# Row dot products on VectorE for a fifth of the w2 and wo blocks, and output 0 moved into the w1 products

## The chip, the cores and the metric

One core of one Trainium2 chip. Times are device microseconds (us) of a whole execution. Single executions of the same kernel lie a few microseconds apart: the kernel before spread over 1172.8 to 1175.9 us in the first job and over 1170.9 to 1181.8 us in the later ones, which ran on three different chips. So a few microseconds are judged here in two ways: by ratios of several runs on the same chip, and by the length of single stages in the profiles.

## The reference

Two layers of one-token attention over a cache of 16384 keys (batch 2, 32 query heads, 4 key/value heads of 128) and an MLP (1024 to 3584 to 1024, GELU), forward and then backward to all inputs and weights. Cut to what the change touches:

```python
x = x + _A_ref(_layernorm(x), k_cache, v_cache, wq, wo)   # layer 0
x = x + _B_ref(_layernorm(x), w1, b1, w2, b2)
x = x + _A_ref(...); x = x + _B_ref(...)                   # layer 1
_out, _vjp = jax.vjp(_f, ...)                              # output 0 is the forward result
_grads = _vjp(grad_out)                                    # 9 gradients
```

In layer 0's backward pass this needs, one after the other, `dh = g @ w2.T` (28 blocks of 128 rows of w2), then the products with w1, two layer-norm backward steps, and `do = g @ wo.T` (32 blocks of wo). Each waits for the result of the one before. After them comes a long last stage that reads the caches again and writes all gradients.

## The kernel before

A weight block arrives as 128 rows on the partitions. For `g @ W.T` TensorE first has to turn it (8 transposes of 128x128 into PSUM), ScalarE or VectorE copies it back (an "eviction"), and 8 small matmuls multiply it. `pick()` and `charge()` balance the evictions between the two engines by an account of their load. For w2 the forward product of layer 1 is done from the same load.

```python
class Ahead:
    def row(self, j):
        w = self.rows[j]
        if self.fps is not None:
            for jo in range(DJ):
                PE.matmul(wide_out(self.fps, jo * WIDE), lhsT=w[:, jo*128:(jo+1)*128], rhs=wide_in(self.x[:, j, :]), ...)
        turn(w, lambda: pt([128, 8, 128], BF16, "turn"))      # 8 transposes and an eviction; 2 PSUM buffers
    def products(self, j, out_ps, gT_bf):
        for o in range(8):
            PE.matmul(wide_out(out_ps, 2 * j), lhsT=self.rows[j][:, o*128:(o+1)*128], rhs=wide_in(gT_bf[:, o, :]), ...)

g2 = attn_in_bwd(1, g3, dn1, lambda: some(rest, 2))           # some(rest, n): row() of the next n blocks
V.tensor_copy(out=gM_all[:, :, lsl(0)], in_=g2[:])
some(rest, 6)
for j in range(FJ):                                           # w2
    some(rest, 1)
    w2b.products(j, dhps, gM_all[:, :, lsl(0)])
mlp_hidden_bwd(0, pairs(dhps, FJ))
x4 = mlp_out(1, ...)
col_to_row_f32(x4, DJ, out_0...)                              # output 0: 8 fp32 transposes, 2 copies, 1 store
_, dmps = w_pass(B_w1, D, F, "dm_ps", gT_bf=dh_all[:, :, lsl(0)])                             # w1
# ... (cut) dm, two ln_bwd with 4 rows of wo turned in each, gA_all ...
for j in range(wob.J + 4):                                    # wo
    some(rest, 1)
    # ... (cut) the last 4 rows ...
    if j >= 4:
        wob.products(j - 4, dops, gA_all[:, :, lsl(0)])
TP = [pt([128, 8, 128], BF16, "tpm%d" % i) for i in range(2)]
for t in TP:
    V.memset(t[:].bitcast(F32), 0.0)
do_delta(0, pairs(dops, HQ))                                  # first instruction: dof
```

## Time and profile before

| | before |
|---|---|
| time, median of the first 3 runs | 1173.21 us (1172.8 to 1175.07) |
| span of the profiled run | 1172.1 us |
| w2 products, first forward to last backward | 673.46 to 700.32 us |
| first w1 transpose; w1 products done (dm_sb) | 703.71; 725.92 us |
| gA_all ready; dof starts | 733.75; 752.05 us |

gM_all and gA_all are the bf16 gradients that the w2 and the wo blocks are multiplied with; dof is the scaled result of wo, with which the last stage begins. In all views PE is TensorE (PEld its weight loads), DVE VectorE, ACT ScalarE and POOL GpSimd; the granted clock (PEclk) is the share of its full clock that TensorE was given.

The windows view of the kernel before, one line for each stage: window, its length, busy us and count of each engine, then granted TensorE clock, DMA share and GB/s.

```profile
core 0: us, PE busy (x) PEld busy (x) DVE busy (x) ACT busy (x) POOL busy (x), PEclk, DMA share, GB/s
673.46:700.32 26.86, 24.40 (x680) 24.09 (x676) 8.93 (x26) 11.15 (x19) 0.00 (x0) 1.00 0.88 317
700.32:703.71 3.39, 1.48 (x9) 0.74 (x10) 1.59 (x7) 0.00 (x0) 0.00 (x0) 0.73 0.94 366
703.71:725.92 22.21, 20.93 (x453) 20.67 (x452) 9.87 (x17) 9.18 (x16) 0.71 (x1) 0.89 0.96 338
725.92:733.75 7.83, 6.25 (x92) 5.46 (x90) 5.51 (x24) 3.02 (x6) 0.00 (x0) 1.00 0.79 291
733.75:752.05 18.30, 16.99 (x424) 16.54 (x423) 8.43 (x14) 6.96 (x12) 0.00 (x0) 1.00 0.71 270
```

TensorE is busy 24.40 of 26.86 us in w2 and 16.99 of 18.30 in wo, VectorE about a third or half of the time. DMA moves 270 to 366 GB/s here, where half of the page's 40 slices show 410 to 423: so in this stretch the time is more likely set by a chain of dependent work. In the second line TensorE is busy 1.48 of 3.39 us: that is output 0. The timeline of TensorE at that place (start, us, engine, line, operation, output<-inputs, idle before and what ended it):

```profile
698.35 1.97 PE L340 MATMUL w2b_b<-gM_all,wt 128*128 128x32 bf16 x72
701.46 0.67 PE L193 MATMUL o<-identf,xM 128*2 128x128 f32 x4 [1.15 <-DVE xM L763]
702.90 1.01 PE L193 MATMUL o<-identf,xM 128*2 128x128 f32 x4 [0.77 <-DVE o_row L194]
703.71 2.77 PE L263 MATMUL wtp<-ident,wt 128*128 128x128 bf16 x24
```

After the last w2 product TensorE waits for x4, makes four fp32 transposes, waits for a copy, makes four more, and only then starts on w1; the granted clock is 0.73 in this gap.

The end of the wo products:

```profile
750.12 1.32 PE L340 MATMUL wob_b<-gA_all,wt 128*128 128x32 bf16 x40
750.32 0.69 DVE L151 COPY wt<-turn 128x1024 bf16<-128x1024 bf16 x1 [0.70 <-PE turn L313]
...
751.12 1.03 DVE L932 MEMSET tpm<- 128x512 f32 x2
752.05 0.22 DVE L803 TENSOR_TENSOR dof<-wob_b,rbc 128x32 f32<-128x32 f32 x2
```

The last products end at 751.44 (750.12 + 1.32), two clearing writes of the transpose buffers take 1.03 us of VectorE, and dof follows.

The cost of a dot is in the profile already, since layer 1's wq products use the same instruction (view of one tile; min, median and max ns):

```profile
L571 DVE SCALAR_TENSOR_TENSOR junk<-wqt,dqb x40: 1206/1217/1226, 561.1 to 660.4; 128x1024 bf16<-128x1024 bf16 x40
L571 DVE DVE_READ_ACCUMULATOR junk<-wqt,dqb x40: 80/82/84, 562.2 to 661.6; 128x1 f32 x40
```

### The profile page before, as it was taken

The numbers are of one execution on the slowest core, as the hardware profiler recorded it, in microseconds if no ns is written. First come the engines' busy times: TensorE is split into PE (matmuls) and PEld (weight loads), VectorE is DVE, ScalarE is ACT, GpSimd is POOL, SyncE is SP. The second block draws the span as 40 slices with busy tenths as digits, with TensorE's granted clock in tenths as the row PEclk, the third lists the DMA queues.
The fourth block names the chain that finished last, engine by engine and source line by source line (L and its number), as shares of the span: only waits on it lengthen the run. The fifth ranks groups of instructions, "written<-read, shape, count | busy, mean of one in ns | idle before, by whom it ended". The sixth has DMA issues, their size and how long they took to land. (4 is left out here: it accounts for less than half of the span.)

```text
span 1172.1 us, 40218 instructions
## 1 busy us (share of the span) xinstructions
PE 968.7 (83%) x17709; PEld 743.1 (63%) x17709; DVE 627.2 (54%) x1319; ACT 555.1 (47%) x1395; POOL 63.9 (5%) x113
## 2 busy tenths in 40 slices
PE   4988885497879876899987889888898999898886
PEld 3866673487767755888775688755555554555452
DVE  1544451133545433454845434567777877886774
ACT  0544441022535430344454434367667867786673
POOL 0000000000000000000000000001111111111111
PEclk9988885587989975999997899888777867887785
DMA  9999999998999989989999989677999999999996
GB/s 370 415 417 416 418 417 396 395 356 351 416 417 413 416 329 416 390 320 398 387 410 411 352 320 338 254 271 322 361 403 419 414 417 421 418 421 418 422 423 263
DMA packets 89131, 449.32 MB, mean 383 GB/s; under 512 B 7026, under 2 KB 7026, under 8 KB 49788
## 3 DMA queue, kind: packets, MB, share of 16 engines
q1 hardware_dynamic: 72204, 348.17, 74.5%
q0 software_dynamic: 16752, 98.59, 20.5%
q8 instruction: 138, 2.26, 0.8%
q14 instruction: 37, 0.30, 0.1%
HBM read 348.14 MB, written 98.58 MB: 381 GB/s over the span
## 5 line engine op out<-in xcount | busy, mean ns | idle before, releaser
L148 ACT COPY kT<-tp 128x512 int32<-128x512 int32 x204 | 120.0, 588 | 254.5 <-PE tp L379 246.6
L151 DVE COPY kT<-tp 128x1024 bf16<-128x1024 bf16 x164 | 112.1, 690 | 117.1 <-PE tp L379 106.9
L379 PE MATMUL tp<-ident,kv_K 128*128 128x128 bf16 x1728 | 144.2, 232 | 4.2 <-DMA kv_K<-in_A_k_cache_dram 4.1
L379 PEld LDWEIGHTS <-kv_K 128*128 128x128 bf16 x1728 | 109.6, 104 | 5.0 <-DMA kv_K<-in_A_k_cache_dram 4.7
L159 DVE CAST big<-xm 128x512 bf16<-128x512 f32 x141 | 91.9, 686 | 33.6 <-PE xm L1018 15.9
L156 ACT CAST big<-xm 128x512 bf16<-128x512 f32 x156 | 84.8, 595 | 24.2 <-PE xm L1018 14.7
L532 PEld LDWEIGHTS <-kT 128*128 128x128 bf16 x2048 | 76.6, 98 | 28.3 <-issue 22.3
L532 PE MATMUL sc<-qT_bf,kT 128*128 128x8 bf16 x2048 | 92.1, 171 | 0.7 <-issue 0.7
L263 PE MATMUL wtp<-ident,wt 128*128 128x128 bf16 x928 | 79.3, 235 | 3.8 <-issue 2.4
L379 PE MATMUL tp<-ident,kv_V 128*128 128x128 bf16 x864 | 72.9, 233 | 9.9 <-DMA kv_V<-in_A_v_cache_dram 8.3
L297 PEld LDWEIGHTS <-wt 128*128 128x128 bf16 x1696 | 48.9, 103 | 45.8 <-issue 14.7
L496 ACT ACTIVATE e_all<-sc,negm 128x64 bf16<-128x64 f32 x256 | 77.2, 345 | 1.1 <-DVE negm L491 1.0
L411 PE MATMUL acc_all<-kv_V,e_all 128*16 128x256 bf16 x864 | 46.4, 295 | 28.4 <-DMA kv_V<-in_A_v_cache_dram 15.4
L148 ACT COPY wT<-wtp 128x512 int32<-128x512 int32 (+1 forms) x60 | 34.5, 576 | 74.1 <-PE wtp L263 65.4
L151 DVE COPY wT<-wtp 128x1024 bf16<-128x1024 bf16 (+1 forms) x64 | 40.5, 637 | 52.7 <-PE wtp L263 49.3
L159 DVE CAST keepK<-xm 128x512 bf16<-128x512 f32 x92 | 59.9, 685 | 16.3 <-PE xm L1159 9.4
L156 ACT CAST keepK<-xm 128x512 bf16<-128x512 f32 x105 | 56.2, 593 | 23.3 <-PE xm L1159 21.1
L379 PEld LDWEIGHTS <-kv_V 128*128 128x128 bf16 x864 | 57.5, 104 | 11.8 <-DMA kv_V<-in_A_v_cache_dram 9.2
L263 PEld LDWEIGHTS <-wt 128*128 128x128 bf16 x928 | 60.7, 105 | 4.6 <-issue 3.1
L156 ACT CAST keepV<-xm 128x512 bf16<-128x512 f32 (+1 forms) x98 | 53.3, 595 | 20.3 <-PE xm L1159 17.0
L496 ACT ACTIVATION_READ_ACCUMULATOR e_all<-sc,negm 128x1 f32 x256 | 60.1, 235 | 0.0
L159 DVE CAST keepV<-xm 128x512 bf16<-128x512 f32 (+1 forms) x74 | 48.5, 686 | 20.3 <-PE xm L1159 16.1
(335 smaller groups left out, 1776.2 us busy)
## 6 DMA issues: line engine op xcount, KB each, us to landing
kv_K<-in_A_k_cache_dram SPq DMA_DIRECT2D x81, 1024.0 KB, 12.9
kv_V<-in_A_v_cache_dram SPq DMA_DIRECT2D x81, 1024.0 KB, 12.6
out_dram<-big POOLq DMA_DIRECT2D x36, 1024.0 KB, 17.7
wt<-in_A_wo_dram SPq DMA_DIRECT2D x32, 1024.0 KB, 11.0
wt<-in_B_w_dram SPq DMA_DIRECT2D x32, 896.0 KB, 14.4
out_dram<-keepK POOLq DMA_DIRECT2D x22, 1024.0 KB, 17.6
out_dram<-keepV POOLq DMA_DIRECT2D x18, 1024.0 KB, 17.7
wt<-in_A_wq_dram SPq DMA_DIRECT2D x16, 1024.0 KB, 9.3
```

The lines of the kernel that those rows point to most:

```text
L148: S.copy(out=dst.bitcast(I32), in_=src.bitcast(I32))
L151: V.tensor_copy(out=dst, in_=src)
L156: S.copy(out=dst, in_=src)
L159: V.tensor_copy(out=dst, in_=src)
L263: PE.transpose(tp[:, o, :], wv[:, j, (o0 + o) * 128:(o0 + o + 1) * 128], ident[:])
L297: PE.matmul(fps[:, jo, :].rearrange("p (a b) -> p a b", b=2), lhsT=wv[:, j, jo * 128:(jo + 1) * 128], rhs=xT_bf[:, j0 + j, :].unsqueeze(1) ...
L379: PE.transpose(tp[:, j, :], cv[:, b * 8 + j, :], ident[:])
L411: PE.matmul(self.acc[cg:cg + 16, :], lhsT=coef(u), rhs=self.cv[:, t:t + 2, :].rearrange("p t d -> p (t d)"), start=False, stop=True, tile_ ...
L496: S.activation(out=e_all[:, g, f * half:(f + 1) * half, l, h, :], in_=sc[g][f][:, h, :].rearrange("p (a b) -> p a b", b=2), func=ACT.Exp, ...
L532: PE.matmul(sc[g][f][:, :, t % TH], lhsT=kT[:, j, :], rhs=q_bf[:, g, :], start=True, stop=True)
```

## The change: intent and diff

TensorE bounds w2 and wo, VectorE has time to spare. For a row block as it lies, `g @ W.T` is a dot product of each partition's row with g. So every fifth block is not turned: VectorE multiplies it with g spread to all partitions and sums along the row, once for each of the 2 batch entries. Spreading g costs 16 transposes and two evictions for each weight. Output 0 leaves in the midst of the w1 products instead of ahead of them. Third, turns of kept V tiles in layer 1 come every third slot instead of every second.

```diff
+    class Dots:                                     # cut
+        def spread(self, b, col):
+            tp = pt([128, 8, 128], BF16, "dotr")
+            for o in range(8):
+                PE.transpose(tp[:, o, :], col(o).to_broadcast([128, 128]), ident[:])
+            evac_bf16(self.rows[b]..., tp..., 1024)
+        def dot(self, w, b, out):
+            V.scalar_tensor_tensor(out=self.junk[:], in0=w, scalar=1.0, in1=self.rows[b]..., op0=ALU.mult, op1=ALU.mult, accum_out=out)
+            charge("D", 1.15)
     class Ahead:
+            self.dotted = range(3, self.J, 5)
+            self.dp = vec.tile([128, len(self.dotted), 2], F32, name=name + "_dp")
-            turn(w, lambda: pt([128, 8, 128], BF16, "turn"))
+            if j not in self.dotted:
+                turn(w, lambda: pt([128, 8, 128], BF16, "turn"))
         def products(self, j, out_ps, gT_bf):
+            if j in self.dotted:
+                for b in range(2):
+                    self.dd.dot(self.rows[j], b, self.dp[:, self.dotted.index(j), b:b + 1])
+                return
-                    if s % 2 == 1 and v_turns:
+                    if s % 3 == 2 and v_turns:
     V.tensor_copy(out=gM_all[:, :, lsl(0)], in_=g2[:])
+    w2b.spread(gM_all[:, :, lsl(0)])
     some(rest, 6)
-    col_to_row_f32(x4, DJ, out_0..., "o0")
-    _, dmps = w_pass(B_w1, D, F, "dm_ps", gT_bf=dh_all[:, :, lsl(0)])
+    _, dmps = w_pass(B_w1, D, F, "dm_ps", gT_bf=dh_all[:, :, lsl(0)],
+                     mid=lambda: col_to_row_f32(x4, DJ, out_0..., "o0"))       # after 4 of 8 chunks
     V.tensor_copy(out=gA_all[:, :, lsl(0)], in_=g1[:])
+    wob.spread(gA_all[:, :, lsl(0)])
# cut: mlp_hidden_bwd (once) and do_delta (once per batch entry) multiply the dotted columns in extra instructions;
# the dots of layer 1's wq products are moved into class Dots unchanged
```

More of the change, by code (lines that the diff above doesn't have):

```diff
@@ L279, in flush, with w_pass @@
                 self.pop()
-    def w_pass(W, n_in, n_out, name, xT_bf=None, gT_bf=None):
+    def w_pass(W, n_in, n_out, name, xT_bf=None, gT_bf=None, mid=None):
         JO, JI = n_out // 128, n_in // 128
@@ L293, in w_pass @@
             wv = w_load(W, j0, rb, n_out)
+            if mid is not None and j0 == 4:
+                mid()
             if fps is not None:
@@ L314, in turn, with __init__ @@
         evac_bf16(view, tp[:].rearrange("p a b -> p (a b)"), 1024)
+    class Dots:
+        def __init__(self, name):
+            self.rows = [ktp.tile([128, 2 * NB, 128], BF16, name=name, tag="blk", bufs=2) for _ in range(2)]
+            self.junk = wrk.tile([128, D], BF16, name="junk", tag="rowout")
+        def spread(self, b, col):
+            tp = pt([128, 8, 128], BF16, "dotr")
+            for o in range(8):
+                PE.transpose(tp[:, o, :], col(o).to_broadcast([128, 128]), ident[:])
+            evac_bf16(self.rows[b][:].rearrange("p a b -> p (a b)"), tp[:].rearrange("p a b -> p (a b)"), 1024)
+        def dot(self, w, b, out):
+            V.scalar_tensor_tensor(out=self.junk[:], in0=w, scalar=1.0, in1=self.rows[b][:].rearrange("p o d -> p (o d)"),
+                                   op0=ALU.mult, op1=ALU.mult, accum_out=out)
+            charge("D", 1.15)
     class Ahead:
@@ L335, in row, with spread @@
                               rhs=wide_in(self.x[:, j, :]), start=False, stop=True, skip_group_check=True)
-            turn(w, lambda: pt([128, 8, 128], BF16, "turn"))
+            if j not in self.dotted:
+                turn(w, lambda: pt([128, 8, 128], BF16, "turn"))
+        def spread(self, gT_bf):
+            self.dd = Dots(self.name + "_g")
+            for b in range(2):
+                self.dd.spread(b, lambda o: gT_bf[:, o, b:b + 1])
         def products(self, j, out_ps, gT_bf):
+            if j in self.dotted:
+                for b in range(2):
+                    self.dd.dot(self.rows[j], b, self.dp[:, self.dotted.index(j), b:b + 1])
+                return
             for o in range(8):
@@ L565, in attn_bwd @@
         dots = deque()
-        dqb = [ktp.tile([128, 2 * NB, 128], BF16, name="dqb", tag="blk", bufs=2) for _ in range(2)]
-        junk = wrk.tile([128, D], BF16, name="junk", tag="rowout")
+        dd = Dots("dqb")
         dnp = vec.tile([128, HKV, DJ, 2], F32, name="dnp")
         def dot(kv, n, j, b):
-            V.scalar_tensor_tensor(out=junk[:], in0=n[4][j - j % 4][:, j % 4, :], scalar=1.0,
-                                   in1=dqb[b][:].rearrange("p o d -> p (o d)"), op0=ALU.mult, op1=ALU.mult,
-                                   accum_out=dnp[:, kv, j, b:b + 1])
-            charge("D", 1.15)
+            dd.dot(n[4][j - j % 4][:, j % 4, :], b, dnp[:, kv, j, b:b + 1])
             if b == 1:
                 V.tensor_tensor(out=dn[:, j], in0=dn[:, j], in1=dnp[:, kv, j], op=ALU.add)
-        def spread(kv, b):
-            tp = pt([128, 8, 128], BF16, "dqr")
-            for o in range(8):
-                PE.transpose(tp[:, o, :], dq_all[:, kv * 8 + o, 2 * l + b:2 * l + b + 1].to_broadcast([128, 128]), ident[:])
-            evac_bf16(dqb[b][:].rearrange("p a b -> p (a b)"), tp[:].rearrange("p a b -> p (a b)"), 1024)
         def by_dots(kv):
@@ L589, in by_dots @@
             for b in range(2):
-                wq_q.append(lambda b=b: spread(kv, b))
+                wq_q.append(lambda b=b: dd.spread(b, lambda o: dq_all[:, kv * 8 + o, 2 * l + b:2 * l + b + 1]))
             def item(j, b):
@@ L764, in mlp_out, with mlp_hidden_bwd @@
         return xn
-    def mlp_hidden_bwd(l, dhps):
+    def mlp_hidden_bwd(l, dhps, ahead=None):
         sv = saved[f"m{l}"]
@@ L781, in mlp_hidden_bwd @@
         V.tensor_tensor(out=dh_all[:, :, lsl(l)], in0=d1[:], in1=dhps[:], op=ALU.mult)
+        if ahead is not None:
+            V.tensor_tensor(out=dh_all[:, 3:FJ:5, lsl(l)], in0=d1[:, 3:FJ:5], in1=ahead.dp[:], op=ALU.mult)
     def mlp_in_bwd(l, gT):
@@ L797, in attn_out_bwd, with do_delta @@
         return do_delta(l, dops)
-    def do_delta(l, dops):
+    def do_delta(l, dops, ahead=None):
         sv = saved[f"a{l}"]
@@ L804, in do_delta @@
                             in1=sv["rbc"][:, b * HKV:(b + 1) * HKV, :].rearrange("p k r -> p (k r)"), op=ALU.mult)
+            if ahead is not None:
+                r_ = sv["rbc"][:, b * HKV:(b + 1) * HKV, :].rearrange("p k r -> p (k r)")
+                V.tensor_tensor(out=dof[:, b * HKV:(b + 1) * HKV, :].rearrange("p k r -> p (k r)")[:, 3:HQ:5],
+                                in0=ahead.dp[:, :, b], in1=r_[:, 3:HQ:5], op=ALU.mult)
         doT_bf = vec.tile([128, G, 8], BF16, name=f"doT_bf{l}")
@@ L906 @@
         w2b.products(j, dhps, gM_all[:, :, lsl(0)])
-    mlp_hidden_bwd(0, pairs(dhps, FJ))
+    mlp_hidden_bwd(0, pairs(dhps, FJ), w2b)
     x4 = mlp_out(1, fps[:, 0:DJ * WIDE].rearrange("p (j b) -> p j b", b=WIDE)[:, :, 0:2])
-    col_to_row_f32(x4, DJ, out_0.rearrange("b s d -> (b s) d"), "o0")
     sv = saved["m0"]
-    _, dmps = w_pass(B_w1, D, F, "dm_ps", gT_bf=dh_all[:, :, lsl(0)])
+    _, dmps = w_pass(B_w1, D, F, "dm_ps", gT_bf=dh_all[:, :, lsl(0)],
+                     mid=lambda: col_to_row_f32(x4, DJ, out_0.rearrange("b s d -> (b s) d"), "o0"))
     wob = Ahead(A_wo, HD, "wob")
@@ L932 @@
         V.memset(t[:].bitcast(F32), 0.0)
-    do_delta(0, pairs(dops, HQ))
+    do_delta(0, pairs(dops, HQ), wob)
     rowsA = ld.tile([128, LDW], BF16, name="rowsA", tag="ld")
```

## The prediction

> **What bounds the kernel now.** The slices show DMA 90% busy or more nearly everywhere (about 415 GB/s when saturated). The windows view shows the exceptions: 317 GB/s in the w2 products (673.5-700.3 us), 338 in the w1 products (703.7-725.9), 246 in the layer-norm chain (725.9-735.2), 293 in the wo products (735.2-752.05), almost nothing at 753-770. There a chain through TensorE decides: PE is busy 24.4 of 26.9 us, 20.9 of 22.2 and 16.1 of 16.85. After about 780 us DMA is saturated again, so what moves the end of that chain (dof at 752.05) should move the kernel's end one for one.
>
> **Removed.** 5 of 28 w2 blocks and 6 of 32 wo blocks lose 8 transposes (0.44 us of PE, start to start), their eviction (0.69 us DVE or 0.59 ACT) and 8 products (0.20): 3.2 us of PE in w2, 3.8 in wo.
>
> **Added.** Two dots per block: in layer 1 the same instruction takes 1.22 us plus a 0.08 us accumulator read, 1.26 start to start. So w2 gets 12.6 us of DVE, wo 15.1. Each stage also gets two spreads (16 transposes, 0.9-1.0 us PE, two evictions) that must wait for gM_all or gA_all; today PE fills that wait with turns.
>
> **w2.** PE waits for gM_all, then spreads: the remaining turns start about 2.5 us later; 3.2 us are saved. The instruction order shows ten dots in one run on DVE, every later eviction on ACT (0.6 us each against 0.85 per row: enough). The dots end about 696-697, before PE. Net gain 0.5-1 us.
>
> **Output 0.** PE stops at 700.32, starts w1 at 703.71, and runs its first 4 us with transposes at about 1.5 times their later time (granted clock 0.73 in the gap, 0.89 over w1, 1.00 before). The Trainium skill ("TensorE: Matmul & The Clock Gate", Part 1) says an idle array falls to a lower clock and needs sustained work to return; this trace agrees. The move removes the gap (3.4 us) and most of the slow start (1.3), and puts about 2.3 us inside w1 (8 fp32 transposes, two copies on one PSUM buffer). Net gain 2.4 us.
>
> **wo.** The spread waits for gA_all and holds both transpose buffers, so the first product comes about 3 us later after gA_all. By the instruction order the twelve dots come in one run after the eviction of row 14: from about 5.6 us after gA_all to 20.7. Two memsets (1.03 us) queue behind, so dof starts about 21.8 us after gA_all, against 18.3 now: DVE becomes the bound, loss 3-4 us. The ln chain loses one turn ahead of it (gain 0.5); extra multiplies cost 0.3.
>
> **Turns of V every third slot** (512-548 us, DMA 332 GB/s, PE 34.9 of 36 us): 5 turns (2.2 us PE) leave this stretch for one nearer DMA's limit. Gain 0-2 us, partly given back at 555-570.
>
> **Sum.** -0.8 -2.4 -0.5 +3.5 +0.3 -0.9 = about -1; allowing somewhat more gain, 1171 us, range 1166 to 1176. Chances: faster by over 2% 0.01, within 2% 0.98, slower by over 2% 0.01.
>
> **What would show it.** w2's first dot near 683; w1's transposes right behind w2's products, clock near 1.0; w1 over about 3 us earlier; wo's dots back to back on DVE, 4 us past PE's last product, so that dof waits for DVE; the idle DMA after wo unchanged in length.
>
> **What would make it wrong.** wo's dots starting earlier (then a gain of 4-5 us); w1's loads held up by buffers that dots free late; a V-turn effect beyond 2 us; the last stage not following the end of wo.

## The result, and the profile after

The changed kernel took 1172.68 us median (1171.82 to 1174.40, 4 runs), the kernel before 1174.14 (1172.80 to 1175.87, 4 runs). The ratio is 0.9989, 95% interval 0.9969 to 1.0008. A ratio here is the mean time of one kernel's runs over that of the other's of the same rounds, so not quite the ratio of the medians.

The same stages in the changed kernel (windows view, columns as above; gap and w1 are one line now):

```profile
672.52:700.17 27.65, 23.57 (x619) 23.01 (x615) 16.77 (x41) 13.36 (x23) 0.00 (x0) 0.93 0.86 319
700.17:723.27 23.10, 20.95 (x461) 20.16 (x459) 9.12 (x20) 10.77 (x19) 0.71 (x1) 0.95 1.01 381
723.27:729.43 6.16, 4.03 (x60) 3.53 (x57) 4.85 (x22) 2.34 (x4) 0.00 (x0) 1.00 0.95 348
729.43:751.97 22.54, 17.44 (x376) 16.51 (x376) 18.36 (x32) 9.95 (x17) 0.00 (x0) 0.89 0.58 216
```

From the start of w2 to gA_all the changed kernel needs 56.9 us (729.43 - 672.52), the one before 60.3 (733.75 - 673.46): 3.4 us less. From gA_all to dof it needs 22.54 us instead of 18.30: 4.2 us more. VectorE's busy time in that last line went from 8.43 to 18.36 us. The reason is in VectorE's timeline there, from gA_all on (three evictions and most of the dots cut):

```profile
729.26 0.17 DVE L951 CAST gA_all<-gM 128x16 bf16<-128x16 f32 x1
730.30 0.69 DVE L151 COPY wob_g<-dotr 128x1024 bf16<-128x1024 bf16 x1 [0.87 <-PE dotr L328]
...
735.08 0.69 DVE L151 COPY wt<-turn 128x1024 bf16<-128x1024 bf16 x1 [0.73 <-PE turn L315]
735.68 1.22 DVE L332 SCALAR_TENSOR_TENSOR junk<-wt,wob_g 128x1024 bf16<-128x1024 bf16 x1
...
737.01 1.23 DVE L332 SCALAR_TENSOR_TENSOR junk<-wt,wob_g 128x1024 bf16<-128x1024 bf16 x1
...
749.69 1.22 DVE L332 SCALAR_TENSOR_TENSOR junk<-wt,wob_g 128x1024 bf16<-128x1024 bf16 x1
750.85 0.08 DVE L332 DVE_READ_ACCUMULATOR junk<-wt,wob_g 128x1 f32 x1
751.03 1.03 DVE L962 MEMSET tpm<- 128x512 f32 x2
751.97 0.17 DVE L827 TENSOR_TENSOR dof<-wob_b,rbc 128x32 f32<-128x32 f32 x1
```

and in TensorE's, which at 729.49 has waited 1.50 us for gA_all, then makes the spread, then four turns, and reaches the first product 4.60 us after gA_all (before: 735.20 - 733.75 = 1.45 us):

```profile
729.49 1.63 PE L328 MATMUL dotr<-ident,gA_all 128*128 128x128 bf16 x16 [1.50 <-DVE gA_all L951]
731.05 3.14 PE L315 MATMUL turn<-ident,wt 128*128 128x128 bf16 x32
734.03 0.56 PE L372 MATMUL wob_b<-gA_all,wt 128*128 128x32 bf16 x16
```

The dots start 6.25 us after gA_all and run back to back to 750.93. TensorE's last product was done at 748.20. The two clearing writes queue behind the dots, and dof waits for both. The stage as measured ends where dof starts; the extra multiplies behind it add to it: from the start of dof to TensorE's first product of the last stage it is 1.10 us (751.97 to 753.07), 0.64 before (752.05 to 752.69).

Output 0's gap is gone, TensorE goes from w2 to w1 at once:

```profile
698.41 1.76 PE L372 MATMUL w2b_b<-gM_all,wt 128*128 128x32 bf16 x61 [1.73 <-issue]
700.01 2.67 PE L263 MATMUL wtp<-ident,wt 128*128 128x128 bf16 x24
```

That line shows a third thing. TensorE stopped for 1.73 us during the last w2 products, for nothing that the profile shows ("issue"), and the granted clock then fell: the 24 transposes took 2.67 us. In a second profile of the same kernel (run e9_after_again) the stop was 1.18 us, the clock stayed at 1.00, and the same 24 took 1.50 us. The length of the stop does not settle it: e10 (no dots, below) stopped for 1.73 us as well, from 685.63 to 687.36 us, and its clock over 687.2 to 700 us was 1.00. Such stops are in all profiles of this stretch, before and after, and scatter by a microsecond or two in sum.

### The profile page after: what moved, and what is told of

Its sections match the earlier page's. It is cut to its first block, busy times and chain, and to the rows that moved or that the text cites. A ratio compares the mean times of both kernels' runs of the same rounds, so it can differ in the third digit from the quotient of the medians.

```text
span 1171.5 us, 39963 instructions
## 1 busy us (share of the span) xinstructions
PE 967.2 (83%) x17565; PEld 738.7 (63%) x17565; DVE 639.2 (55%) x1342; ACT 562.9 (48%) x1412; POOL 63.7 (5%) x113
## 3 DMA queue, kind: packets, MB, share of 16 engines
q0 software_dynamic: 16752, 98.59, 20.5%
## 5 line engine op out<-in xcount | busy, mean ns | idle before, releaser
L159 DVE CAST big<-xm 128x512 bf16<-128x512 f32 (+1 forms) x137 | 89.4, 686 | 27.2 <-PE xm L1189 12.4
L156 ACT CAST big<-xm 128x512 bf16<-128x512 f32 (+1 forms) x160 | 87.1, 593 | 25.1 <-PE xm L1048 13.3
L411 PE MATMUL tp<-ident,kv_V 128*128 128x128 bf16 x864 | 69.8, 227 | 9.7 <-DMA kv_V<-in_A_v_cache_dram 8.4
L299 PEld LDWEIGHTS <-wt 128*128 128x128 bf16 x1696 | 49.1, 104 | 44.6 <-issue 14.9
L148 ACT COPY wT<-wtp 128x512 int32<-128x512 int32 (+1 forms) x63 | 36.1, 575 | 70.4 <-PE wtp L263 60.3
L156 ACT CAST keepK<-xm 128x512 bf16<-128x512 f32 x103 | 55.6, 592 | 22.1 <-PE xm L1189 20.5
L263 PEld LDWEIGHTS <-wt 128*128 128x128 bf16 x928 | 60.3, 105 | 5.1 <-issue 3.8
```

Of the source, the lines that this page charges most:

```text
L148: S.copy(out=dst.bitcast(I32), in_=src.bitcast(I32))
L156: S.copy(out=dst, in_=src)
L159: V.tensor_copy(out=dst, in_=src)
L263: PE.transpose(tp[:, o, :], wv[:, j, (o0 + o) * 128:(o0 + o + 1) * 128], ident[:])
L299: PE.matmul(fps[:, jo, :].rearrange("p (a b) -> p a b", b=2), lhsT=wv[:, j, jo * 128:(jo + 1) * 128], rhs=xT_bf[:, j0 + j, :].unsqueeze(1) ...
L411: PE.transpose(tp[:, j, :], cv[:, b * 8 + j, :], ident[:])
```

## The experiments

Theory T: up to the end of the w1 products and the layer norms the change gains; the wo dots give it back, because they start late and VectorE then needs 15.2 us for them. Rivals: R1, the last stage is bound by its own bytes and does not follow an earlier dof; R2, the stages gained nothing and the wo dots cost nothing. All experiments are edits of the changed kernel unless said otherwise, all gave correct results, and each was timed in 6 runs against 11 runs of the kernel before on the same chip. Three jobs and a last one: e1 to e4; e5 to e8; e9 to e11; e12.

Stage lengths, read from the timelines: "w2" from the first forward product to the last backward one, "to dm" from there to the copy of w1's result (so with output 0's gap), "ln" to gA_all ready, "wo" to the start of dof, all in us.

| run | w2 | to dm | ln | wo | sum | dof at | dof to end | ratio to before (95%) |
|---|---|---|---|---|---|---|---|---|
| before | 26.86 | 25.60 | 7.83 | 18.30 | 78.59 | 752.05 | 420.05 | |
| e11 before again | 26.29 | 24.02 | 7.82 | 18.29 | 76.42 | 751.28 | 424.42 | 1.0000 (0.9976-1.0024) |
| e12 before, tiles shifted | 26.30 | 24.29 | 7.83 | 18.29 | 76.71 | 750.41 | 422.49 | 1.0008 (0.9983-1.0033) |
| changed | 27.65 | 23.10 | 6.16 | 22.54 | 79.45 | 751.97 | 419.53 | 0.9989 (0.9969-1.0008) |
| e9 changed again | 26.33 | 21.01 | 6.16 | 22.68 | 76.18 | 748.70 | 423.40 | 0.9962 (0.9939-0.9985) |
| e1 no wo dots | 27.06 | 20.73 | 7.28 | 18.29 | 73.36 | 746.25 | 419.15 | 0.9961 (0.9936-0.9986) |
| e2 no w2 dots | 27.95 | 20.46 | 6.58 | 22.49 | 77.48 | 749.17 | 422.43 | 0.9982 (0.9961-1.0003) |
| e3 output 0 back | 25.97 | 26.35 | 6.17 | 21.77 | 80.26 | 755.60 | 420.00 | 1.0015 (0.9995-1.0036) |
| e4 V turns back | 26.28 | 22.11 | 6.32 | 22.42 | 77.13 | 749.92 | 422.68 | 1.0003 (0.9977-1.0029) |
| e5 clearing on ScalarE | 26.79 | 21.56 | 6.17 | 20.64 | 75.16 | 747.89 | 422.61 | 0.9965 (0.9939-0.9991) |
| e6 late spreads | 26.15 | 21.01 | 6.27 | 20.63 | 74.06 | 747.65 | 421.25 | 0.9959 (0.9936-0.9981) |
| e7 as e8, 4 wo dots | 25.95 | 21.01 | 6.27 | 17.52 | 70.75 | 744.88 | 421.82 | 0.9932 (0.9902-0.9962) |
| e8 all early | 25.09 | 21.67 | 6.27 | 18.25 | 71.28 | 743.33 | 421.27 | 0.9930 (0.9904-0.9956) |
| e10 no dots at all | 27.39 | 22.50 | 7.82 | 17.72 | 75.43 | 748.33 | 424.07 | 0.9958 (0.9933-0.9982) |

### e1: no dots in wo

```diff
-    wob = Ahead(A_wo, HD, "wob")
+    wob = Ahead(A_wo, HD, "wob", dotted=range(0))     # no block dotted, no spread
```

> The changed kernel with the wo dots undone (all 32 wo blocks turned and multiplied on TensorE, no spread); w2 dots, moved output 0 and V turns kept. Theory T (the gain up to the end of the w1 products is real and the wo dots give it back on VectorE): the span from gA_all to dof falls from 22.5 us to about 18.3, dof starts near 748 instead of 752, and the kernel ends about 3.7 us earlier, near 1169. Rival R1 (the last stage is bound by its own bytes and does not follow): dof near 748 but the time stays at 1172 to 1173. Rival R2 (the product stages gained nothing, the wo dots cost nothing): dof stays at 752.

The wo stage is 18.29 us, the length of before to a hundredth, and dof comes at 746.25. The median was 1170.68 us, the ratio 0.9961. The end of the stage in this run: the clearing writes follow a single eviction instead of twelve dots.

```profile
744.52 0.69 DVE L151 COPY wt<-turn 128x1024 bf16<-128x1024 bf16 x1 [1.34 <-PE turn L315]
745.32 1.02 DVE L965 MEMSET tpm<- 128x512 f32 x2
746.25 0.22 DVE L830 TENSOR_TENSOR dof<-wob_b,rbc 128x32 f32<-128x32 f32 x2
```

T holds in the stage, R2 falls. The whole time is clearly below the kernel before, but against the changed kernel (0.9989 and 0.9962 in two jobs) single ratios are too wide to settle 4 us; R1 is judged below from all the runs together.

### e2: no dots in w2

```diff
-    w2b = Ahead(B_w2, F, "w2b", h_all[:, :, lsl(1)], fps)
+    w2b = Ahead(B_w2, F, "w2b", h_all[:, :, lsl(1)], fps, range(0))
```

> The changed kernel with the w2 dots undone, the rest kept. The traces put the w2 stage, first forward product to last backward product, at 26.9 us before and 27.5 after. T as the traces suggest (the wait for gM_all and the spread eat all of it): the w2 stage is about 0.6 us shorter than in the changed kernel and the time about 1172. As the prediction had it (w2 dots gain 0.5 to 1 us): about 1173.5.

The w2 stage was not shorter but 27.95 us, against 27.65 and 26.33 in the two profiles of the changed kernel; the ratio 0.9982 against 0.9989 and 0.9962. Both expectations are inside the scatter. In e10, also without w2 dots, it was 27.39; the kernel before and its two copies, without them too, took 26.29 to 26.86. So the w2 dots as placed in the change are worth between nothing and about a microsecond.

### e3: output 0 ahead of the w1 products again

```diff
+    col_to_row_f32(x4, DJ, out_0.rearrange("b s d -> (b s) d"), "o0")
-    _, dmps = w_pass(B_w1, D, F, "dm_ps", gT_bf=dh_all[:, :, lsl(0)], mid=lambda: col_to_row_f32(x4, ...))
+    _, dmps = w_pass(B_w1, D, F, "dm_ps", gT_bf=dh_all[:, :, lsl(0)])
```

> The changed kernel with output 0 put back in front of the w1 products. T: the gap of about 3.4 us on TensorE between the w2 and the w1 products is back, the w1 products start at a lower granted clock, their end comes 2.3 us later, and the kernel ends 2.3 us later, near 1175. R1 or R2: no change, 1172.7.

```profile
699.61 1.70 PE L372 MATMUL w2b_b<-gM_all,wt 128*128 128x32 bf16 x61 [0.21 <-issue]
703.73 1.01 PE L193 MATMUL o<-identf,xM 128*2 128x128 f32 x4 [2.42 <-DVE xM L785]
705.52 1.01 PE L193 MATMUL o<-identf,xM 128*2 128x128 f32 x4 [0.77 <-DVE o_row L194]
706.32 2.77 PE L263 MATMUL wtp<-ident,wt 128*128 128x128 bf16 x24
```

The gap is back and longer than before, 5.01 us: the w2 dots ended only at 701.29, so the chain for x4 on VectorE stood behind them (TensorE waited 2.42 us for xM, 1.15 before). The way from w2 to dm is 26.35 us, against 20.5 to 23.1 in the ten profiles with output 0 moved (mean 21.5) and 24.0 to 25.6 in the three of the kernel before and its copies (mean 24.6). The median was 1176.95 us, the ratio 1.0015, the highest ratio of all. Moving output 0 is worth 3 us between w2 and dm, more with the dots in place.

### e4: V turns every second slot again

```diff
-                    if s % 3 == 2 and v_turns:
+                    if s % 2 == 1 and v_turns:
```

> The changed kernel with the turns of V back in every second slot. In the changed kernel the w2 stage starts 0.94 us earlier than before. T: that comes from the turns, so the w2 stage starts near 673.5 again and the time is near 1173.6. Rival: it is a difference between runs, and the start stays near 672.5 and the time at 1172.7.

The w2 stage started at 672.79, the median was 1175.30 and the ratio 1.0003, nominally slower than the changed kernel. From layer 1's dof, just ahead of the V turns, to the start of w2 the four profiles with turns every second slot take 163.7 to 164.4 us (mean 164.1), the ten with every third 162.2 to 165.4 (mean 163.9). (The first V turn is no fair start: with every third slot it comes later itself.) A gain of 0.2 us would fit, nothing would too. This part stays open.

### e5: the clearing writes on ScalarE

```diff
-        V.memset(t[:].bitcast(F32), 0.0)
+        S.activation(out=t[:].rearrange("p a b -> p (a b)").bitcast(F32), in_=onesf[:, 0:1].to_broadcast([128, 512]), func=ACT.Copy, scale=0.0)
```

> The changed kernel with only the two clearing writes of the transpose buffers moved from VectorE (where they queue behind the last dot, 1.03 us) to ScalarE, idle there. T: dof follows the last dot directly, 1 us earlier, about 1171.7. If the dots were not what dof waits for, nothing changes.

The wo stage is 20.64 us instead of 22.5 to 22.7, and dof follows the last dot directly at 747.89. That is 1.9 us, not 1.0: the dots also started 5.49 us after gA_all instead of 6.25 (732.74 - 727.25). The granted clock in that stretch was 1.00 here (windows view, 727.25 to 733.00), and 0.73 in both profiles of the changed kernel (729.43 to 735.68; 726.02 to 732.42). The windows of the changed kernel and of e5, then e5's last dot and dof:

```profile
729.43:735.68 6.25, 6.19 (x88) 5.81 (x89) 2.68 (x5) 1.75 (x3) 0.00 (x0) 0.73 0.04 14
727.25:733.00 5.75, 4.89 (x91) 4.51 (x92) 2.94 (x6) 1.98 (x4) 0.00 (x0) 1.00 0.21 78
```

```profile
746.74 1.22 DVE L332 SCALAR_TENSOR_TENSOR junk<-wt,wob_g 128x1024 bf16<-128x1024 bf16 x1
747.89 0.08 DVE L332 DVE_READ_ACCUMULATOR junk<-wt,wob_g 128x1 f32 x1
747.89 0.18 DVE L827 TENSOR_TENSOR dof<-wob_b,rbc 128x32 f32<-128x32 f32 x1
```

So about 1.0 us is the clearing, and the rest goes with the clock: e3, also at 1.00 there, started its dots 5.49 us after gA_all too. (In e4, at 1.00, they started at 6.14, with the evictions dealt to the engines in another order, so the clock is not all.) The clock's scatter has a visible side. In both profiles of the changed kernel and in e2 it fell to 0.50 within 2 us of the end of TensorE's 1.5 us wait for gA_all; in e3, e4 and e5 the same wait passed without a fall; in e6, e7 and e8, where turns stand ahead of the spread and TensorE's wait at that place is 0.67 us, the clock stayed at 1.00 until the dots. Dof did wait for VectorE.

### e6: both spreads later

```diff
-    w2b.spread(gM_all[:, :, lsl(0)])
     some(rest, 6)
+    w2b.spread(gM_all[:, :, lsl(0)])
...
+    some(rest, 5)
     wob.spread(gA_all[:, :, lsl(0)])
-    for j in range(wob.J + 4):
-        some(rest, 1)
+    for j in range(4, wob.J + 4):
+        if j > 4:
+            some(rest, 1)
```

> The changed kernel with both spreads issued later on TensorE: after the six w2 blocks and after five more wo blocks, so that the turns fill the wait for gM_all and gA_all as in the kernel before. Same instructions, other order. T: the 1.5 us waits of TensorE before both spreads go; in w2 about 1.5 us are gained; in wo the dots start about 3.7 us after gA_all instead of 6.2 and dof comes about 2.6 us earlier: in all near 1168.6. If the spread's place does not matter: 1172.7.

The wo stage is 20.63 us: the dots start 4.36 us after gA_all (731.38 - 727.02) and dof comes 1.9 to 2.1 us earlier than in the two profiles of the changed kernel, somewhat less than the 2.6 expected. The w2 stage was 26.15 us, a small gain over 26.33 and 27.65 where 1.5 was expected. The median was 1170.90, the ratio 0.9959. The place of the spread matters in wo. Some of the gain goes through the clock, which was 1.00 here: against e3's 21.77 us, with the old place and the same clock, it is 1.1 us.

### e7 and e8: late spreads, dots first, clearing on ScalarE

```diff
 # e6, e5, and the dots leave products() for a loop position three blocks earlier:
+        w2b.dots(j + 3)
         w2b.products(j, dhps, gM_all[:, :, lsl(0)])
...
+            wob.dots(j - 4 + 3)
             wob.products(j - 4, dops, gA_all[:, :, lsl(0)])
 # e7 only: 4 wo blocks as dots instead of 6
+    wob = Ahead(A_wo, HD, "wob", dotted=range(3, 19, 5))
```

> Late spreads as in e6, the clearing writes on ScalarE, the dots issued three blocks ahead of their turn, and only 4 of 32 wo blocks as dots (10.1 us of VectorE instead of 15.1). T: VectorE ends about 14 us after gA_all, TensorE about 15, dof about 15.3 instead of 22.5; with 1.5 us from w2 the kernel ends near 1164. R1 (the last stage does not follow): above 1170.

> As e7 but with all 6 wo blocks as dots (15.1 us of VectorE). T: VectorE is the bound again, its dots end about 18.9 us after gA_all, dof about 19, the kernel near 1167.6, some 3.5 us later than e7. If TensorE were the bound, e8 would be earlier than e7 by up to 1.3 us, which is what two blocks fewer on TensorE are worth.

The ends of the wo stage on VectorE, first e8, then e7:

```profile
742.17 1.22 DVE L332 SCALAR_TENSOR_TENSOR junk<-wt,wob_g 128x1024 bf16<-128x1024 bf16 x1
743.33 0.08 DVE L332 DVE_READ_ACCUMULATOR junk<-wt,wob_g 128x1 f32 x1
743.33 0.18 DVE L830 TENSOR_TENSOR dof<-wob_b,rbc 128x32 f32<-128x32 f32 x1
```

```profile
740.92 1.23 DVE L332 SCALAR_TENSOR_TENSOR junk<-wt,wob_g 128x1024 bf16<-128x1024 bf16 x1
742.07 0.08 DVE L332 DVE_READ_ACCUMULATOR junk<-wt,wob_g 128x1 f32 x1
744.88 0.19 DVE L833 TENSOR_TENSOR dof<-wob_b,rbc 128x32 f32<-128x32 f32 x1 [2.73 <-PE wob_b L373]
```

In e8 dof follows the last dot, so VectorE is the bound, as expected. In e7 VectorE was idle for 2.73 us and waited for the last product, so there TensorE is the bound, as expected too. But the difference between them was missed: e7 needed 17.52 us where 15.3 was expected, because TensorE's products took 14.9 us from first to last (729.97 to 744.85) and began 2.61 us after gA_all. So e7 and e8 are equal: wo 17.52 and 18.25 us, medians 1166.89 and 1166.59, ratios 0.9932 and 0.9930. Both beat the kernel before. Their stage sums (70.75 and 71.28 us) beat both profiles of the changed kernel (79.45 and 76.18), with dots that start 3.1 us after gA_all instead of 6.25; in the whole time their intervals lie below the changed kernel's first one (0.9969 to 1.0008) but overlap e9's (0.9939 to 0.9985), which is of another job.

### e9, e10, e11: controls, and no dots at all

e9 is the changed kernel and e11 the kernel before, unaltered; e10 is the changed kernel without any dot and with the clearing on ScalarE (edits of e1, e2 and e5).

> The changed kernel once more, unaltered, as a control for how far one profile differs from the next. In the eight experiments the w2 stage starts between 671.7 and 675.3 us and dof to the end takes 419.2 to 422.7 us. If that is the difference between executions: gA_all to dof is 22.5 us again within 0.2, while dof to the end may lie anywhere in that range; the time against the kernel before is 0.999 within 0.003.

> The kernel before, unaltered, profiled on the same chip as the others: control. gA_all to dof 18.3 us, the gap in front of the w1 products 3.4 us; ratio 1.000 within 0.003. Where its w2 stage starts tells whether the 0.94 us between the first two profiles belong to the V turns: if it lies within the range of the changed kernels, 671.7 to 675.3 us, they need not.

> No dots in w2 or wo at all; output 0 amid the w1 products, V turns every third slot, clearing writes on ScalarE. It tells what the dots are worth where they are placed well (e8: ratio 0.993). Sum of the parts: gA_all to dof 17.7 to 18.3 us, w2 stage 26.9 to 28, ratio about 0.9965. If the dots were worth nothing even in e8: 0.993.

The wo stages repeated to 0.14 us (22.54 and 22.68; 18.30 and 18.29), as did the layer norms (6.16; 7.83 and 7.82). The last stage did not: the same program needed 419.53 and 423.40 us from dof to the end, the kernel before 420.05 and 424.42. So no single profile can say what moved the last stage by less than about 4 us. e10, with medians 1170.99 against 1176.55 and a ratio of 0.9958, shows that as much as the whole gain of the changed kernel could be had without dots (it also has the clearing on ScalarE, which its wo stage of 17.72 us shows): its sum of stages is 75.43 us, the changed kernel's 79.45 and 76.18. Against e8's 71.28 us the dots are worth about 4 us in the stages where they are placed well, less the 0.4 us of extra multiplies behind dof. In the whole time this is not clear of noise: the ratios 0.9958 and 0.9930 come from different jobs, and their intervals overlap.

### Does the last stage follow?

With the fourteen profiles of the table, the end of the span lies between 419.2 and 424.4 us after dof, while dof itself moves from 743.33 to 755.60 us. A straight line through the ends against dof has slope 0.94, with a scatter of 1.6 us about it. That is a fit, worked out from the table; the standard error of the slope is 0.15. R1 would have a slope near zero. Dof also moves with whatever came before w2, but the end against the sum of the four stages alone has a slope of 0.99 with an error of 0.20. R1 falls; within its scatter the end moves one for one with dof.

### e12: the kernel before with its tiles shifted

All eleven profiles of changed programs (the expectation, written too low, says nine) reached the sum of layer 0's MLP hidden units 0.8 to 1.1 us earlier than the two of the kernel before, although up to there no instruction differs in kind or order. What differs is where tiles lie: the small result tiles of the dots move every larger SBUF tile by up to 128 bytes.

```diff
 # kernel before:
+            self.pad = vec.tile([128, len(range(3, self.J, 5)), 2], F32, name=name + "_pad")
+            V.memset(self.pad[:], 0.0)
```

> The kernel before plus two small unused tiles (40 and 48 bytes per partition, cleared once) in the pool where the changed kernel puts the results of its dots, so that every larger tile of SBUF lies 128 bytes further on, at the addresses of the changed kernel; nothing else. In both profiles of the kernel before, layer 0's MLP hidden sum ends at 230.0 us, in all nine of the changed kernel and its variants so far at 228.9 to 229.2, though up to there no instruction differs. If the addresses do that: about 229.1 us here, the gA_all to dof span 18.3 us as before, and a ratio of about 0.998. If not: 230.0 us and 1.000 within 0.003.

One line each of the view of this tile, kernel before, e12 and changed kernel; the first of the two start times is layer 0:

```profile
L741 DVE TENSOR_TENSOR hpre<-acc_all,b1T x2: 216/216/217, 230.0 to 457.6; 128x56 f32<-128x56 f32 x2
```

```profile
L743 DVE TENSOR_TENSOR hpre<-acc_all,b1T x2: 216/217/218, 229.1 to 456.7; 128x56 f32<-128x56 f32 x2
```

```profile
L763 DVE TENSOR_TENSOR hpre<-acc_all,b1T x2: 217/218/218, 229.2 to 456.8; 128x56 f32<-128x56 f32 x2
```

230.0, 229.1 and 229.2 us: in this one profile the shift alone gives the 0.9 us up to there. The median of e12 was 1175.16 against 1174.37 us, ratio 1.0008: nothing of it is visible in the whole time. Why the address matters was not tested; it is also not known whether 128 bytes are special, since the two result tiles of e10 have 8 bytes each instead of 40 and 48, so that it moved the tiles by less, and it was as early.

## Why the prediction was right

The time was right (1171 predicted with 1166 to 1176; 1172.68 measured), and so was the main step: what is gained up to gA_all is given back in wo. The exact number owes something to luck: output 0 and the layer norms gained about 1.9 us more than predicted, the w2 dots 0.5 to 1 us less, and wo lost 0.7 to 0.9 us more, and these errors nearly cancel. Nor does the number alone say much: the range also holds the 1174.14 us of a change that does nothing. What speaks for the prediction is the course of the wo stage, and e1.

| step | predicted | measured |
|---|---|---|
| w2 dots | 0.5 to 1 us gained | within scatter: w2 27.65 and 26.33 us with, 27.95 and 27.39 without (e2, e10), 26.29 to 26.86 in the kernel before and its copies |
| output 0 moved | 2.4 us gained | about 3.1 us: w2 to dm 21.5 us mean of ten, 24.6 mean of three |
| layer norms | 0.5 us gained | 1.67 us (7.83 to 6.16) |
| wo, gA_all to dof | from 18.3 to about 21.8 us | 22.54 and 22.68 us |
| extra multiplies | 0.3 us lost | 0.46 us from dof to the next product (1.10 and 0.64) |
| V turns | 0 to 2 us gained | 0.2 us in the means, not settled |
| last stage follows dof | one for one | slope 0.94 over fourteen profiles |

- **w2.** TensorE waited 1.51 us for gM_all and the spread took 1.07 us, as the prediction reckoned; the dots ended at 697.48 us, ahead of TensorE, as said. The first dot came at 684.79, not near 683. The saving of 3.2 us of TensorE is just about eaten up.
- **Output 0.** The gap is gone and the clock over w1 is 0.95 in the first profile; in e9 it was 1.00 from the first transpose. The Trainium skill ("TensorE: Matmul & The Clock Gate", "Wait — 56ns, not 53.3ns?") gives 55.6 ns from one matmul of 128 columns to the next at the full clock and 106.7 ns while the array is cold. This trace shows the same for transposes of 128 columns: a turn of 8 at a granted clock of 1.00 takes 0.44 us to the next instruction (55 ns each), and 24 right after the gap of before, at 0.50, took 703.71 to 706.27, 107 ns each. The prediction's "about 1.5 times" fits the duration of a single transpose (311 and 219 ns); from start to start it is 1.9 times.
- **Layer norms.** The term was undersized. The first sum came 0.5 us earlier, as predicted for the turn that is missing ahead of it (2.23 us after dm_sb before, 1.71 after: 728.15 - 725.92 and 724.98 - 723.27). The remaining 1.1 us lie between the first and the second sum (3.40 and 2.67 us), where before TensorE waited 0.67 us for an eviction on ScalarE, and between that and gA_all (2.20 and 1.78), where before a VectorE eviction of 0.69 us stood ahead of the sum's use. The term belongs mostly to the wo dots: without them the norms took 7.28 us (e1), without any dots 7.82 (e10).
- **w1 and DMA.** In the first pair of profiles the copy of w1's result came at 723.27 instead of 725.92 us, 2.65 us earlier (predicted: about 3). After wo, from 753 to 770 us, DMA moved 186 GB/s at a share of 0.45 before and 184 at 0.44 after, unchanged as predicted.
- **wo.** First product 3.15 us later after gA_all than before (4.60 and 1.45; predicted 3), dots from 6.25 us after gA_all to 21.5 (predicted 5.6 and 20.7), dof at 22.54 (21.8). The dots ended 2.7 us after TensorE's last product, not 4, because TensorE was late as well.
- **The allowance for "somewhat more gain"** had no reason behind it, and the first profiled pair needed none of it: its spans are 1172.1 and 1171.5 us. The ratio of 0.9962 in the job of e9 would fit it, but the stage sums of that job (76.42 and 76.18 us) differ by only 0.2 us, so where it comes from stays open.

## What to carry to other kernels

Work taken from a busy engine helps only if the engine that takes it over can start early: here the idle VectorE got 15 us of dots that could start only after a spread which waited on the critical result, and a clearing write queued behind them. Fill the wait for a critical value with independent work and put the spread behind it, start the moved work first, and move small instructions off the queue it fills: together that turned a change of 0.1 to 0.4% into one of 0.7%. Cost a move from the time its input is ready to the time its consumer starts, on the new engine, and look at what else stands in that queue.

## What the Trainium skill lacked or had wrong

- "TensorE: Matmul & The Clock Gate", Part 1, puts the fall of the clock after an idle window of about 3.4 us, free-running, and the section "Why this matters for your kernels" names only gaps over about 3 us as harmful. Here the granted clock fell from 1.00 (698.41 to 699.10 us) to 0.50 (699.10 to 702.51 us, 3.41 us long) just after a TensorE stop of 1.73 us (changed kernel), so a stop of half the page's window was followed by a fall; the 24 transposes then took 2.67 us instead of e9's 1.50. It stayed at 1.00 after a stop of 1.18 us (e9) and also after another of 1.73 us (e10), so the length of the stop alone does not decide. A free-running window, which a stop can straddle, would explain that; no run here tests it, nor how much of a window must be idle.
- No page that I found tells of an effect of a tile's SBUF address on speed: with the tiles shifted by 128 bytes the first 230 us were 0.9 us shorter (e12, one profile). "DMA: Bandwidth & Descriptors", "How a descriptor splits into AXI transactions", tells what a read that does not start 256-byte aligned costs; a load here writes its tile, and no run tells whether the address of a load is the cause.
- "VectorE: DVE Perf Modes" has no time for a multiplication with a sum along the row. Here it takes 1.22 us for 1024 bf16 elements plus 0.08 us for reading the sum, 1.27 us start to start.
